# Gated mix of two attention branches, forward and backward: the token stage of the memory branch on the 32x32 blocks of each segment, with compact stores

## The chip, the core and the metric

One core of a Trainium2 chip. The metric is the device time of one launch in microseconds (us), the median of several runs; lower is better. Engines: TensorE (PE, with its weight loads PEld), VectorE (DVE), ScalarE (ACT), GpSimd (POOL) and SyncE (SP, which here only issues DMAs; POOL and ACT issue some too). Each engine takes its instructions in order.

## What is computed

The reference is a forward pass with all its gradients (12 outputs). Two branches read the same x of 2048 tokens with 576 features:

```python
a = _A_ref(x, ...)          # 32 query heads of 18, one key and one value head, softmax over all 2048 tokens
b = _B_ref(x, mem0, ...)    # 32 heads of 128, 64 segments of 32 tokens, one after the other
return g * a + (1 - g) * b  # g = sigmoid(sum(x * gate_w))
```

Branch B is where the change lies. Per segment it computes

```python
h = concatenate([mem, xs])                          # 8 memory rows + 32 tokens
q, k, v = h @ Wq, h @ Wk, h @ Wv                    # per head, 128 wide
scores = where(mask, q @ k.T * scale, -1e9)         # 40 x 40; mask: memory keys always, tokens causal
o = softmax(scores) @ v @ Wo
mem = o[:8]; outs.append(o[8:])                     # the next segment's memory
```

So a token sees 8 memory keys and at most 32 token keys, those of its own segment. The backward pass needs, for each segment and head, P (the softmax), dP = dO v^T less the row sum of dO times o, dS = scale * P * dP, and dq = dS k, dk = dS^T q, dv = P^T dO.

## The kernel before, in words

The program runs in stages: preparation and projections; the forward memory chain (segment by segment, for the memory rows alone), woven with the first pass of branch A; **the token stage** (`b_bulk`); the backward memory chain (`b_chain_bwd`), woven with the second pass of branch A; the backward token stage (`b_post`); the weight gradients (`b_dw`); the end of branch A. Within these stages the order of work on each engine is the order in which the program writes it; a DMA load may be issued somewhat earlier.

*Token stage, `b_bulk`.* 2048 tokens are 16 tiles of 128 rows, that is of 4 segments. A unit of work t (128 of them) is one tile and 4 heads; a chunk is 4 units (16 heads), and loads and stores go by chunks: q, dO, k with four buffers, v with three (L678). A software pipeline runs over ticks. In tick t the list `order` calls one step after the other, each for the unit t - n:

```python
order = [(0, st_QT), (1, st_S), (3, st_T), (4, st_O), (0, st_KT), (2, st_R), (1, st_M), (5, st_OT), (5, st_VT),
         (6, st_D), (0, st_GT), (7, st_B), (8, st_DT), (9, st_Q), (7, st_K)]
```

- `st_QT`, `st_KT`, `st_GT`, `st_VT`, `st_OT`: 4 transposes each on PE (helper `tr`, L87) of q, k, dO, v and o into a PSUM tile `x_tr` (two buffers), copied out by DVE (q, k; L77) or ACT (v, dO at L79, o at L789). `st_OT` also multiplies dO and o on POOL (`x_prod`, L792).
- `st_S`: scores. Per head one product of 128 queries with all 128 keys of the tile (`x_S`; helper `mm`, L82), though three quarters of it belong to other segments, and one with the 4 x 8 memory keys (`x_m`). Two exponentials on ACT (L751, L752) write `x_E`, 160 columns a head.
- `st_M` sets to zero what lies outside the segment and above the diagonal, with a bit mask of 160 columns (DVE, L757). `st_R`: row sums (DVE, L764), reciprocal (L766), P and its memory part Pm (POOL, L769). P with all 128 columns goes to DRAM as `px_dram`.
- `st_T`, `st_DT`: transpose P (and dS). DVE transposes the 4 x 128 columns in 32x32 blocks (L713), which is the whole transpose since only diagonal blocks are not zero; PE transposes the memory part, ACT copies it.
- `st_O`, `st_Q` (through `attend`): o and dq into `x_po` (one buffer): one product of 512 columns with the memory rows in block-diagonal form (`mB`), 4 products of the full 128 x 128 blocks; ACT copies (L723).
- `st_D`: dP into `x_D` as 4 products dO v^T and 4 with a matrix of -1 that subtract the row sums, the same for the memory part in `x_m`; DVE makes dS and dSm (L828); dS goes to DRAM as `dsx_dram`.
- `st_B`: output projection, 8 products of 288 columns. `st_K`: in every second tick 16 products in 32-column tiles for the memory rows' dk and dv (`x_m`; ACT copies `x_dm`, L856).

Stores are collected and issued on SP a tick later (`flush`, L706).

*Who reads the stored blocks.* In `b_chain_bwd`, `kv_load` brings P and dS for the four heads of a step (`r_ks`, L1011), the left operand of the dk and dv products of the last 11 tiles, and `load_a` brings v of the next segment with a transposing DMA (`r_vxT`, L953). In `b_post`, `load` brings P and dS (`y_p`, `y_ds`, L1231) for the first 6 tiles, 8 heads at a time, with three buffers; `y_q` and `y_dO` come beside them (L1233), and `load_s` (L1216, L1219) the memory rows' part.

Of the kernel before, what the change touches and what calls it, by code (L numbers as in the profile page):

```python
# [9 lines left out]
ACT = mybir.ActivationFunctionType  # L10
# [36 lines left out]
class Kern:  # L47
# [52 lines left out]
    def setup_B_dram(self, dram):  # L100
# [20 lines left out]
        self.px_dram = t("px_dram", [NTT, P, HB, P])  # L121
        self.dsx_dram = t("dsx_dram", [NTT, P, HB, P])
# [8 lines left out]
    def setup_B_consts(self, pool):  # L131
# [16 lines left out]
        mz = pool.tile([P, 160], F32, name="maskZ")  # L148
        nc.gpsimd.memset(mz[:], 0.0)
        for sl in range(4):  # L150
            r = slice(32 * sl, 32 * sl + 32)
            nc.gpsimd.memset(mz[r, 32 * sl:32 * sl + 32], 65535.0)
            nc.gpsimd.memset(mz[r, P + 8 * sl:P + 8 * sl + 8], 65535.0)
        nc.gpsimd.affine_select(out=mz[:, 0:P], in_=mz[:, 0:P], compare_op=ALU.is_ge, fill=0.0,
                                base=0, pattern=[[-1, P]], channel_multiplier=1)
        mx = pool.tile([P, 160], U16, name="maskX")
        nc.vector.tensor_copy(mx[:], mz[:])
        self.maskX = mx
        ng = pool.tile([P, 160], BF16, name="negones")
# [485 lines left out]

    def b_bulk(self, wp, lp, sp, psum):
# [49 lines left out]
        def store(t, dst, src):  # L696
            if t % 4 == 3:
                tt, h0 = t // 8, 16 * (t // 4 % 2)
                if len(dst.shape) == 4:
                    due[1].append((dst[tt][:, h0:h0 + 16, :], src[:]))  # L700
                else:
                    due[1].append((dst[tt * P:(tt + 1) * P, h0 * P:h0 * P + 2048], src[:].rearrange("p h e -> p (h e)")))
# [24 lines left out]
        def trans(t, w, nb):  # L727
            tt, g, r, d = view(t)
            pt = psum.tile([P, 5, P], BF16, name="x_tr", bufs=2)
            for i in range(4):  # L730
                self.tr(pt[:, i, :], d[w][:, 4 * (g % 4) + i, :], P)
            o = sp.tile([P, 4, P], BF16, name=f"x_{w}T", bufs=nb)
            self.evac(o[:], pt[:, 0:4, :], use="s" if w in ("dO", "v") else "v")
            sc[w + "T", t] = o
# [6 lines left out]
        def st_S(t):  # L741
            tt, g, r, d = view(t)
            qT4, kT4 = sc.pop(("qT", t)), sc.pop(("kT", t))
            Sp = psum.tile([P, 4, P], F32, name="x_S", bufs=1)
            Sm = psum.tile([P, 4, 32], F32, name="x_m", bufs=1)
            for i in range(4):
                self.mm(Sp[:, i, :], lhsT=qT4[:, i, :], rhs=kT4[:, i, :], start=(i == 0), stop=True)
            for i in range(4):
                self.mm(Sm[:, i, :], lhsT=qT4[:, i, :], rhs=mT[tt]["k"][:, :, 4 * g + i, :], start=(i == 0), stop=True)
            Et = sp.tile([P, 4, 160], BF16, name="x_E", bufs=3)  # L750
            nc.scalar.activation(Et[:, :, 0:128], Sp[:], ACT.Exp, scale=SCALEB)  # L751
            nc.scalar.activation(Et[:, :, 128:160], Sm[:], ACT.Exp, scale=SCALEB)  # L752
            sc["E", t] = Et

        def st_M(t):
            Et = sc["E", t]
            nc.vector.tensor_tensor(out=Et[:].bitcast(U32), in0=Et[:].bitcast(U32),  # L757
                                    in1=mx[:].bitcast(U32).unsqueeze(1).to_broadcast([P, 4, 80]), op=ALU.bitwise_and)

        def st_R(t):  # L760
# [3 lines left out]
            nc.vector.tensor_reduce(out=l[:], in_=Et[:], axis=AX.X, op=ALU.add)  # L764
            rl = sp.tile([P, 4], F32, name="x_r", bufs=2)
            nc.vector.reciprocal(rl[:], l[:])  # L766
            for w, lo, n in (("P", 0, 128), ("Pm", 128, 32)):
                o = chunk(t, w, [P, 16, n], 3)
                nc.gpsimd.tensor_tensor(out=o[:, r, :], in0=Et[:, :, lo:lo + n],  # L769
                                        in1=rl[:].unsqueeze(2).to_broadcast([P, 4, n]), op=ALU.mult)  # L770
            store(t, self.px_dram, d["P"])

        def st_T(t):
            tt, g, r, d = view(t)
            sc["PT", t] = transp(d["P"][:, r, :], d["Pm"][:, r, :], "x_PT", "s")

        def st_O(t):
            tt, g, r, d = view(t)
            o = chunk(t, "o", [P, 16, P], 2)
            attend(o[:, r, :], sc.pop(("PT", t)), mB["v"][t // 4 % 2][:, g % 4], d["v"][:, r, :])  # L780
# [15 lines left out]
        def st_B(t):  # L796
            tt, g, r, d = view(t)
            oT = sc.pop(("oT", t))
            if g == 0:
                pb[tt] = psum.tile([P, 2, 512], F32, name="x_b", bufs=1)  # L800
            for i in range(4):
                for hf in range(2):
                    self.mm(pb[tt][:, hf, 0:288], lhsT=oT[:, i, :], rhs=self.WoN[:, 4 * g + i, 288 * hf:288 * hf + 288],
                            start=(g == 0 and i == 0), stop=(g == 7 and i == 3))
            if g == 7:
# [5 lines left out]
        def st_D(t):  # L811
            tt, g, r, d = view(t)
            prod = sc.pop(("prod", t))
            dOT4 = sc.pop(("dOT", t))
            vT4 = sc.pop(("vT", t))
            dP = psum.tile([P, 4, P], F32, name="x_D", bufs=1)
            dM = psum.tile([P, 4, 32], F32, name="x_m", bufs=1)
            for i in range(4):
                self.mm(dP[:, i, :], lhsT=dOT4[:, i, :], rhs=vT4[:, i, :], start=(i == 0), stop=False)
            for i in range(4):  # L820
                self.mm(dP[:, i, :], lhsT=prod[:, i, :], rhs=self.negones[:, 0:128], start=False, stop=True)
            for i in range(4):
                self.mm(dM[:, i, :], lhsT=dOT4[:, i, :], rhs=mT[tt]["v"][:, :, 4 * g + i, :], start=(i == 0), stop=False)
            for i in range(4):
                self.mm(dM[:, i, :], lhsT=prod[:, i, :], rhs=self.negones[:, 0:32], start=False, stop=True)
            for w, p, src, n in (("dS", "P", dP, 128), ("dSm", "Pm", dM, 32)):
                o = chunk(t, w, [P, 16, n], 2)
                nc.vector.scalar_tensor_tensor(out=o[:, r, :], in0=src[:], scalar=SCALEB,  # L828
                                               in1=d[p][:, r, :], op0=ALU.mult, op1=ALU.mult)
# [1275 lines left out]
```

## Time and profile before

| | |
|---|---|
| runs | 5593.44 us median of 3 (5592.29 to 5598.78) |
| profiled execution | span 5569.0 us from the first to the last instruction; what the runs' median has beyond it is 24.4 us |
| granted PE clock | 0.979 mean; 1.00 in most of the token stage |
| token stage | first scores at 2135.4 us, last at 2775.2 us |
| backward memory chain with pass 2 | some 2810 to 4530 us |
| backward token stage | first product 4536.6 us, last 4774 us |
| weight gradients, end of branch A | from 4788.6 us |

Lines of the profile name the source line, the engine, the operation and the tiles (out<-in). "128*32" ahead of a shape is the part of the PE array in rows and columns that an instruction uses; a product's own length is its way through the array, and products overlap, so start-to-start times tell what one costs.

### The profile page before, as it was taken

Reading aid. Unit: us, or ns where it says so; the run is one execution under the profiler, and the core shown is the slowest. Engines: PE = TensorE matmul, PEld = TensorE weight load, DVE = VectorE, ACT = ScalarE, POOL = GpSimd, SP = SyncE. Lnnn points to the kernel's source line nnn. Section 1 sums busy time; section 2 is a strip of 40 time slices with the busy share of each in tenths; the row PEclk is TensorE's granted clock in tenths of the full one; section 3 lists DMA queues with packets and bytes.
Section 4 is the critical chain, followed back from the end, with each engine's and each line's share of the span. In section 5 each row is a group of like instructions: output and inputs, shape, how many; then the busy total and the mean of one; then the engine's idle time right before and its main releaser. Section 6 shows DMA issues by size and latency. Waiting matters only on the chain. (4 is left out here: it accounts for less than half of the span.)

```text
span 5569.0 us, 204829 instructions
## 1 busy us (share of the span) xinstructions
PE 5231.2 (94%) x87117; PEld 2909.5 (52%) x87117; DVE 3726.0 (67%) x6818; ACT 3506.8 (63%) x5266; POOL 2297.4 (41%) x4320
## 2 busy tenths in 40 slices
PE   7999999999999998999969999999998889899999
PEld 6434444444444445777734555555544457674444
DVE  5337888888888887888868888888888821121111
ACT  4327888788878886888857878878877732111101
POOL 4004555555555545555514544444543421122213
PEclk9999999999999998999979999999999999999999
DMA  6646666766675546888765999999987679876653
GB/s 214 220 173 136 136 138 137 137 138 133 144 135 117 119 99 192 258 256 253 233 228 156 199 200 208 213 202 212 215 181 146 138 181 250 244 214 229 209 165 115
DMA packets 1109896, 1012.49 MB, mean 182 GB/s; under 512 B 666386, under 2 KB 919067, under 8 KB 1099378
## 3 DMA queue, kind: packets, MB, share of 16 engines
q1 hardware_dynamic: 1004706, 747.39, 56.4%
q0 software_dynamic: 100736, 247.10, 14.4%
q8 instruction: 681, 11.16, 0.9%
q10 hardware_dynamic: 3536, 4.90, 0.3%
q14 instruction: 237, 1.94, 0.1%
HBM read 547.90 MB, written 383.13 MB: 167 GB/s over the span
## 5 line engine op out<-in xcount | busy, mean ns | idle before, releaser
L1684 DVE TENSOR_TENSOR a_W<-a_dP,a_E 128x512 bf16<-128x512 f32 x2048 | 1315.1, 684 | 269.9 <-issue 128.7
L1824 DVE TENSOR_TENSOR b_dS<-b_dP,b_E 128x512 bf16<-128x512 f32 x2048 | 1311.8, 684 | 249.3 <-issue 109.0
L1801 ACT ACTIVATE b_E<-b_S 128x1024 bf16<-128x1024 f32 x1024 | 1048.3, 1024 | 308.2 <-PE b_dP L82 237.0
L1654 ACT ACTIVATE a_E<-a_S 128x1024 bf16<-128x1024 f32 x1024 | 1050.0, 1025 | 255.8 <-PE a_dP L82 166.5
L82 PEld LDWEIGHTS <-b_QS 32*128 32x128 bf16 (+1 forms) x8192 | 258.0, 92 | 564.9 <-issue 521.4
L82 PE MATMUL r_pj<-WT,r_dT 128*32 128x288 bf16 x12288 | 496.7, 289 | 17.0 <-issue 16.5
L82 PE MATMUL b_S<-b_KV,b_QS 32*128 32x512 bf16 x2048 | 409.1, 390 | 96.8 <-ACT b_E L1801 77.7
L82 PE MATMUL w_acc<-w_d,w_h 128*128 128x512 bf16 (+1 forms) x2400 | 473.8, 379 | 0.0
L82 PE MATMUL a_S<-a_QD,l_KV 32*128 32x512 bf16 x2048 | 400.3, 384 | 39.5 <-ACT a_E L1654 34.9
L82 PE MATMUL b_acc<-b_dS,b_QS 128*32 128x512 bf16 x2048 | 430.8, 399 | 0.7 <-DVE b_dS L1824 0.5
L82 PE MATMUL b_dP<-b_KV,b_QS 32*128 32x512 bf16 x2048 | 409.8, 394 | 8.2 <-DVE b_dS L1824 8.2
L82 PE MATMUL a_acc<-a_W,l_WK 128*32 128x512 bf16 x4096 | 414.5, 390 | 2.7 <-issue 2.4
L82 PE MATMUL b_acc<-b_E,b_QS 128*32 128x512 bf16 x2048 | 412.8, 400 | 0.0
L82 PE MATMUL a_acc<-a_E,l_VK 128*32 128x512 bf16 x4096 | 405.0, 381 | 5.8 <-issue 1.1
L82 PE MATMUL a_dP<-a_QD,l_KV 32*128 32x512 bf16 x2048 | 399.2, 386 | 0.0
L82 PEld LDWEIGHTS <-r_dT 128*32 128x32 bf16 x12288 | 333.8, 97 | 114.8 <-issue 24.0
L82 PEld LDWEIGHTS <-w_h 128*128 128x128 bf16 (+1 forms) x2688 | 229.8, 100 | 258.8 <-issue 6.9
L82 PEld LDWEIGHTS <-hm 128*32 128x32 bf16 x7680 | 203.9, 97 | 195.0 <-issue 0.8
L769 POOL TENSOR_TENSOR x_P<-x_E,x_r 128x512 bf16<-128x512 bf16 x128 | 152.7, 1193 | 293.6 <-DVE x_r L766 293.6
L79 ACT CAST w_o<-w_acc 128x512 bf16<-128x512 f32 x54 | 31.6, 585 | 384.3 <-PE w_acc L82 365.0
L77 DVE CAST w_o<-w_acc 128x512 bf16<-128x512 f32 x54 | 37.3, 691 | 333.4 <-PE w_acc L82 306.5
L82 PEld LDWEIGHTS <-l_KV 32*128 32x128 bf16 x4096 | 122.0, 91 | 250.6 <-issue 206.2
(461 smaller groups left out, 10953.2 us busy)
## 6 DMA issues: line engine op xcount, KB each, us to landing
b_QS<-qs_dram SPq DMA_DIRECT2D x256, 256.0 KB
dOx_dram<-p_tok SPq DMA_DIRECT2D x16, 1024.0 KB
c_vx<-vx_dram SPq DMA_DIRECT2D x64, 256.0 KB
krow_dram<-c_k POOLq DMA_DIRECT2D x64, 256.0 KB
qrow_dram<-c_q POOLq DMA_DIRECT2D x64, 256.0 KB
vrow_dram<-c_v POOLq DMA_DIRECT2D x64, 256.0 KB
x_q<-qx_dram SPq DMA_DIRECT2D x32, 512.0 KB
x_dO<-dOx_dram SPq DMA_DIRECT2D x32, 512.0 KB
```

The source lines that it names most:

```text
L77: nc.vector.tensor_copy(out, in_)
L79: nc.scalar.copy(out, in_)
L82: return self.nc.tensor.matmul(out, lhsT, rhs, start=start, stop=stop, tile_position=tp, skip_group_check=True)
L769: nc.gpsimd.tensor_tensor(out=o[:, r, :], in0=Et[:, :, lo:lo + n], in1=rl[:].unsqueeze(2).to_broadcast([P, 4, n]), op=ALU.mult)
L1654: nc.scalar.activation(E_[n][:], S.pop(n)[:], ACT.Exp, scale=SCALEA)
L1684: nc.vector.tensor_tensor(out=W_[n][:, i, :], in0=dP[i][:], in1=E_[n][:, i, :], op=ALU.mult)
L1801: nc.scalar.activation(E_[n][:], S.pop(n)[:], ACT.Exp, scale=SCALEA)
L1824: nc.vector.tensor_tensor(out=D_[n][:, i, :], in0=dP[i][:], in1=E_[n][:, i, :], op=ALU.mult)
```

## The change

Scores, dP, P and dS of a segment's tokens are computed, kept and stored as 32x32 blocks only. In detail:

- Scores and dP go to one PSUM tile `x_SD` of one bank, for both the score unit (t - 1) and the dP unit (t - 6) of a tick: the memory products and the row-sum products first (`st_SDm`, full array; the row-sum product now covers token and memory columns at once, 64 columns), then per head and segment a product of 32 queries with 32 keys in one of four 128x32 tiles of the array (`st_SDx`, 32 products).
- `x_E`, P and dS have 32 token and 32 memory columns a head: one exponential, one mask, one sum, one multiplication on POOL, one dS on DVE.
- o and dq: the memory product as before (`attend_m`, all full-array products of a tick together), then per head and segment a 32x32 block times 32 rows, at the array position (32c, 32c) (`attend_x`, 32 products in a tick for both). `x_po` has two buffers.
- Steps are split and sorted so that products of one mode stand together, and the projection's 8 products stand in pairs between the transposes. DVE copies dO's transposes and the two small ones (P, dS), ACT no longer does.
- P and dS are stored as `pd_dram` (32 columns a head). The transposed v is kept by chunk and stored as `vT_dram`, four stores a chunk.
- `b_chain_bwd` loads v's transpose from `vT_dram` with a plain DMA, and P and dS together with four DMAs (one a segment) into the diagonal blocks of two tiles that POOL has set to zero at its start. `b_post` does the same for `y_p` and `y_ds` with four DMAs each, into three tiles each, cleared by POOL and DVE at its start.

```diff
-        self.px_dram = t("px_dram", [NTT, P, HB, P])
-        self.dsx_dram = t("dsx_dram", [NTT, P, HB, P])
+        self.pd_dram = t("pd_dram", [NTT, P, 2, HB, SEG])
+        self.vT_dram = t("vT_dram", [NSEG, P, HB, SEG])
...
+    def load_diag(self, dst, tt, hs, w=slice(0, 2)):
+        for i in range(4):
+            r = slice(32 * i, 32 * i + 32)
+            self.nc.sync.dma_start(dst(r), self.pd_dram[tt][r, w, hs, :])
...
-        def transp(x, m, nm, use):
+        def transp(d, r, nm):
             pt = psum.tile([P, 5, P], BF16, name="x_tr", bufs=2)
-            self.tr(pt[:, 0, :], m.rearrange("p i t -> p (i t)"), P)
-            o = sp.tile([P, 640], BF16, name=nm, bufs=2)
-            nc.vector.transpose(o[:, 0:512], x.rearrange("p i t -> p (i t)"))
-            self.evac(o[:, 512:640], pt[:, 0, :], use=use)
+            self.tr(pt[:, 0, :], d[:, 1, r, :].rearrange("p i t -> p (i t)"), P)
+            o = sp.tile([P, 256], BF16, name=nm, bufs=2)
+            nc.vector.transpose(o[:, 0:128], d[:, 0, r, :].rearrange("p i t -> p (i t)"))
+            nc.vector.tensor_copy(o[:, 128:256], pt[:, 0, :])
             return o
-        def attend(o, PT, m, v):
-            po = psum.tile([P, 4, P], F32, name="x_po", bufs=1)
-            self.mm(po[:].rearrange("p i e -> p (i e)"), lhsT=PT[:, 512:640], rhs=m.rearrange("p i e -> p (i e)"),
+        def attend_m(PT, m):
+            po = psum.tile([P, 4, P], F32, name="x_po", bufs=2)
+            self.mm(po[:].rearrange("p i e -> p (i e)"), lhsT=PT[:, 128:256], rhs=m.rearrange("p i e -> p (i e)"),
                     start=True, stop=False)
+            return po
+        def attend_x(o, po, PT, v):
             for i in range(4):
-                self.mm(po[:, i, :], lhsT=PT[:, 128 * i:128 * i + 128], rhs=v[:, i, :], start=False, stop=True)
+                for c in range(4):
+                    r32 = slice(32 * c, 32 * c + 32)
+                    self.mm(po[r32, i, :], lhsT=PT[r32, 32 * i:32 * i + 32], rhs=v[r32, i, :],
+                            start=False, stop=True, tp=(32 * c, 32 * c))
             nc.scalar.copy(o, po[:])
...
+            if w == "v":
+                o = chunk(t, "vT", [P, 4, 16, SEG], 2)
+                nc.scalar.copy(o[:, :, r, :].rearrange("p s h t -> p h s t"),
+                               pt[:, 0:4, :].rearrange("p h (s t) -> p h s t", t=SEG))
+                if t % 4 == 3:
+                    for c in range(4):
+                        due[1].append((self.vT_dram[4 * tt + c][...], o[:, c]))
+                return
-            self.evac(o[:], pt[:, 0:4, :], use="s" if w in ("dO", "v") else "v")
+            nc.vector.tensor_copy(o[:], pt[:, 0:4, :])
...
-        def st_S(t):
...
-            for i in range(4):
-                self.mm(Sp[:, i, :], lhsT=qT4[:, i, :], rhs=kT4[:, i, :], start=(i == 0), stop=True)
...
+        def seg_mm(dst, lT, rT, first):
             for i in range(4):
+                for c in range(4):
+                    r32 = slice(32 * c, 32 * c + 32)
+                    self.mm(dst[r32, 0, i, :], lhsT=lT[:, i, r32], rhs=rT(i, c), start=False, stop=True, tp=(0, 32 * c))
+        def st_SDm(tick):
+            SD[tick] = psum.tile([P, 2, 2, 4, SEG], F32, name="x_SD", bufs=1)
...
+                    self.mm(SD[tick][:, 0, 1, i, :], lhsT=sc["qT", t][:, i, :], rhs=mT[tt]["k"][:, :, 4 * g + i, :], ...)
...
+                    self.mm(dP[:, 1, i, :], lhsT=dOT4[:, i, :], rhs=mT[tt]["v"][:, :, 4 * g + i, :], ...)
...
+                    self.mm(dP[:, :, i, :], lhsT=prod[:, i, :], rhs=self.negones[:]...)
+        def st_SDx(tick):
...
+                seg_mm(SD[tick][:, 0], qT4, lambda i, c: kT4[:, i, 32 * c:32 * c + 32], True)
+                Et = sp.tile([P, 2, 4, SEG], BF16, name="x_E", bufs=3)
+                nc.scalar.activation(Et[:], SD[tick][:, 0], ACT.Exp, scale=SCALEB)
...
+                seg_mm(SD[tick][:, 1], sc.pop(("dOT", t)), lambda i, c: vT[:, c, 4 * (t % 4) + i, :], False)
+                o = chunk(t, "dS", [P, 2, 16, SEG], 2)
+                nc.vector.scalar_tensor_tensor(out=flat(o[:, :, r, :]), in0=flat(SD[tick][:, 1]), scalar=SCALEB,
+                                               in1=flat(d["P"][:, :, r, :]), op0=ALU.mult, op1=ALU.mult)
+                store_pd(t, 1, d["dS"])
...
-        order = [(0, st_QT), (1, st_S), (3, st_T), (4, st_O), (0, st_KT), (2, st_R), (1, st_M), (5, st_OT), (5, st_VT),
-                 (6, st_D), (0, st_GT), (7, st_B), (8, st_DT), (9, st_Q), (7, st_K)]
+        B_ = lambda i: lambda t: st_B(t, i)
+        order = [(0, st_QT), (7, B_(0)), (0, st_KT), (7, B_(1)), (5, st_OT), (7, B_(2)), (5, st_VT), (7, B_(3)),
+                 (0, st_GT), (4, st_Om), (9, st_Qm), (3, st_T), (None, st_SDm), (8, st_DT), (2, st_R), (7, st_K),
+                 (None, st_SDx), (1, st_M), (4, st_Ox), (9, st_Qx)]
...
-            nc.sync.dma_start_transpose(L["vxT"][:], self.xtok["v"][s * 32:(s + 1) * 32, :])
+            nc.sync.dma_start(L["vxT"][:], self.vT_dram[s])
...
+        kvA = [kvp.tile([P, 2, 4, P], BF16, name=f"r_ks{i}") for i in range(2)]
+        for t in kvA:
+            nc.gpsimd.memset(t[:], 0.0)
...
-            a = kvp.tile([P, 4, P], BF16, name="r_ks", bufs=3)
-            nc.sync.dma_start(a[:], (self.dsx_dram if w else self.px_dram)[tt][:, 4 * g:4 * g + 4, :])
+                self.load_diag(lambda r: kvA[n // 2 % 2][r, :, :, r], tt, slice(4 * g, 4 * g + 4))
...
+        PD = {w: [pool.tile([P, 8, P], BF16, name=f"y_{w}{i}") for i in range(3)] for w, pool in (("ds", rp), ("p", sp))}
+        for i in range(3):
+            nc.vector.memset(PD["ds"][i][:], 0.0)
+            nc.gpsimd.memset(PD["p"][i][:], 0.0)
...
+                if w in PD:
+                    d[w] = PD[w][c % 3]
+                    for i in range(4):
+                        r = slice(32 * i, 32 * i + 32)
+                        nc.sync.dma_start(d[w][r, :, r], self.pd_dram[tt][r, int(w == "ds"), h0:h0 + 8, :])
+                    continue
```

More of the change, by code (lines that the diff above doesn't have):

```diff
@@ L809, in st_B, with st_Qm, st_Qx @@
                 due[1].append((self.b_dram[tt * P:(tt + 1) * P, :], b[:].rearrange("p a b -> p (a b)")))
[L811 to L829, printed above, removed]
[L830 removed]
         def st_DT(t):
             tt, g, r, d = view(t)
[L834 to L836 removed]
+            sc["DT", t] = transp(d["dS"], r, "x_DT")
+        def st_Qm(t):
+            tt, g, r, d = view(t)
+            sc["pq", t] = attend_m(sc["DT", t], mB["k"][t // 4 % 2][:, g % 4])
+        def st_Qx(t):
             tt, g, r, d = view(t)
             dq = chunk(t, "dq", [P, 16, P], 2)
[L839 removed]
+            attend_x(dq[:, r, :], sc.pop(("pq", t)), sc.pop(("DT", t)), d["k"][:, r, :])
             store(t, self.xtok["dq"], dq)
@@ L1966, in build_full @@
             k.setup_A_consts(cpool)
-            k.setup_B_consts(cpool)
+            k.setup_B_consts(cpool, a1s)
             k.load_Wo(bwo)
```

136 lines of the change are left out of this document (79 added, 57 removed).

## The prediction, made before the changed kernel was built

> **What bounds the kernel now.** I read the page first, then the stage table (busy time by window), then the token stage's tiles, its groups by form and its timeline, and last the waits and SP's timeline of the two later stages that read what is stored.
>
> ```profile
> span 5569.0 us, 204829 instructions
> ...
> PE 5231.2 (94%) x87117; PEld 2909.5 (52%) x87117; DVE 3726.0 (67%) x6818; ACT 3506.8 (63%) x5266; POOL 2297.4 (41%) x4320
> ```
>
> The span is 24.4 us under the runs' median of 5593.4; I take that rest as unchanged and add all differences to the median. 0.2% of it, 11 us, is about what a measurement of this kernel can tell from no change. PE is busy everywhere, so the question is what PE does in the stage that is changed.
>
> ```profile
> core 0: us, PE busy (x) PEld busy (x) DVE busy (x) ACT busy (x) POOL busy (x), PEclk, DMA share, GB/s
> ...
> 2300.00:2400.00 100.00, 92.64 (x1423) 76.01 (x1423) 83.03 (x181) 82.48 (x190) 52.12 (x60) 1.00 0.83 256
> ```
>
> ```profile
> L82 PE MATMUL x_S<-x_kT,x_qT x512: 218/219/315, 2135.4 to 2775.2; 128*128 128x128 bf16 x171
> ```
>
> The 128 groups ("ticks") of the token stage take 2775.2 - 2135.4 = 639.8 us for 127 steps: 5.04 us a tick, at full granted clock. PE leads, DVE and ACT are at 83%, the DMA engines too. The timeline of PE shows what a product costs and where PE stands still (start, length, operation, how many):
>
> ```profile
> 2404.88 0.39 PE L82 MATMUL x_po<-x_k,x_DT 128*128 128x128 bf16 x4
> ...
> 2405.20 0.25 PE L82 MATMUL x_m<-x_q,x_dSm 128*32 128x128 bf16 x4
> ...
> 2405.26 0.24 PE L82 MATMUL x_m<-x_dO,x_Pm 128*32 128x128 bf16 x4
> ...
> 2405.37 0.24 PE L82 MATMUL x_m<-x_dO,x_Pm 128*32 128x128 bf16 x4
> ...
> 2405.55 0.40 PE L87 MATMUL x_tr<-identB,x_q 128*128 128x128 bf16 x4
> ...
> 2407.92 0.38 PE L87 MATMUL x_tr<-identB,x_v 128*128 128x128 bf16 x4 [0.28 <-DVE x_kT L77]
> ```
>
> Four full products with 128 columns end their stream after 4 x 0.056 = 0.22 us (0.39 less the 0.22 of one, over 3 steps: 0.056 each). Four products in 32-column tiles start together and the next four 0.057 later: 0.014 us each. Between the modes there is a hole: the first tiled product could start at 2405.11 and starts at 2405.20, the first full one after them could at 2405.43 and starts at 2405.55. From the single start times one change of mode costs 0.095 us. The last line is a standstill: the transpose of v needs a buffer that DVE has not emptied.
>
> Adding up the start-to-start times of 100 ticks gives 4.15 us of streaming in a tick (42 products of 128 columns, 2.35; 12 of 32 columns at 0.025, 0.30; 8 of 288 columns at 0.122, 0.98; 2 of 512 at 0.216, 0.43; 8 tiled, 0.11) and 0.89 of standing: 0.36 before v's transposes, 0.20 before the memory scores, 0.11 before `x_po`, 0.10 before o's transposes, 0.10 in mode changes.
>
> **The change, step by step.**
>
> *PE's streaming.* 22 transposes stay (1.23), the output projection (0.98), the two 512-column products (0.43), the tiled key products (0.11), 8 memory products of 32 columns (0.20). Four products with 128 columns and four with 32 become four with 64: between 0.025 and 0.056 each, nearer the short ones, 0.12. The 4 + 4 full score products become 32 of 32 columns in 128x32 tiles. Their nearest row is the memory chain's:
>
> ```profile
> 2089.67 0.39 PE L82 MATMUL a_S<-a_QD,l_KV 32*128 32x512 bf16 x2
> 2089.67 0.39 PE L82 MATMUL a_dP<-a_QD,l_KV 32*128 32x512 bf16 x2
> 2089.99 0.40 PE L82 MATMUL a_acc<-a_W,l_WK 128*32 128x512 bf16 x4
> ...
> 2090.65 0.41 PE L82 MATMUL c_x<-c_qT,c_kmT 128*8 128x8 bf16 x32
> ```
>
> 32 column-tiled products of 8 columns take 0.41 less one tail of 0.17: 0.0075 us each. 32 columns need hardly more: 0.23 a tick, and at most 0.80 if each held the array for the 0.025 of a 32-column full product. [...]
>
> The 8 products of 128 columns in attention output and dq become 32 in 32x32 tiles on the diagonal, 4 beside each other: 0.014 each as in the column tiles, 0.45. No row has this mode. That four row groups can run together the first two lines above show (four starts within 0.01 us), but each of those writes a PSUM bank of its own, and here four row groups write one. Upper bound: one after the other, 32 x 0.056 = 1.79. I take 0.45, since the diagonal's four write different partitions as the column tiles do. [...]
>
> Sum 3.75. Sorted by mode there are 3 changes a tick (full, 128x32, 32x32, full): 0.29. PE: 4.03 us.
>
> *The other engines.* DVE: the two 128x512 transposes (0.70) shrink to 128x128 (between the 0.20 of `r_xq`, 128x64, and 0.435 of `r_pq`, 128x256: 0.28), the reduce from 640 to 256 elements (0.81 to 0.41 at 1.04 ns each), mask 0.46 to 0.26, dS 0.68 + 0.28 to 0.41; it gains dO's copy (0.42) and two small copies (0.20 each) from ACT. Sum of the rows 4.65 to 3.5. ACT loses those copies and one exponential: 4.7 to 3.1. POOL 2.75 to 1.8. None reaches 4.03.
>
> *What is late next.* With the projection spread between the transposes, PE reaches dO's transposes 1.87 after q's. They need o's buffer: o's transposes end at 1.32, ACT's copy (0.59) ends at 1.95, so 0.12 of standing; in every second tick ACT has also the 0.59 of `x_dm` and runs late by another 0.12. DVE's row from dO's copy to the next q copy (0.34 + 0.36 + 0.36 + 0.51 + 0.33 + 0.18 + 0.42, starts overlapping by 0.08) plus the 1.32 from o's to dO's transposes and the hand-overs is 4.05: just about PE's length, another 0.05 to 0.1 in odd ticks. Tick: 4.2, and 4.25 with the chunk borders. 5.04 - 4.25 = 0.79, times 128 is 101 us; the 9 filling and emptying ticks give half of that, 4 us.
>
> *DMA and SP in this stage.* By the trace's packet records the 16 engines work 4.19 us a tick. Two stores with 128 rows of 4 KB a chunk of four ticks go (64 packets a tick at 201 ns over 16 engines: -0.80), six with 128 rows of 1 KB come (192 at 46 to 62 ns: +0.55 to 0.74): 3.94 to 4.13 a tick, less than 4.25 but close; that is rival B. SP issues four more stores a chunk, 4 x 0.4 = 1.6 us beside 11.5 of 17: hidden; if not, 0.4 a tick.
>
> *Backward memory chain (2810 to 4530).* v comes by a plain load instead of a transposing one (SP 1.6 to 0.45, 64 times) and each pair of blocks by 4 DMAs of 64-byte runs instead of 2 (88 x 2 x 0.5 more on SP): +15 us of SP's time in 1700. 90112 packets of 64 bytes at the 11 ns of the 72-byte ones are 62 us of 16 engines for 87 removed. PE's waits for DMA there sum to under 4 us in 1630, so I take 0, bounds -5 and +15. Two memsets on POOL at the start: +1.
>
> *Backward token stage (4537 to 4774).* Six more DMAs a chunk, 3 us of SP beside idle stretches of 6.5 in 9.6: hidden. But its start hangs on SP: `y_p` went out at 4523.8, the twelve loads behind it, and PE waited 11.0 us for the last. Now POOL must clear the first tile after its last chain DMA (4527) and more loads go ahead: +6, bounds 0 to 15.
>
> Forecast: 5593.4 - 101 - 4 + 1 + 6 = 5495 us.
>
> **The rivals.**
> B, DMA-bound token stage: 4.04 us of transfers at a share of 0.88 (just above the stage's 0.85 now) is a tick of 4.6: -56 - 4 + 7, 5540. Against it: shares up to 1.00 in the backward token stage.
> C, slower: the diagonal products run one by one. 1.79 for 0.45 makes the tick 4.25 + 1.34 = 5.59, and 5.55 where some standing is hidden by it: +65 + 7, 5665. It decides from about 0.040 us a product on. For it: no row shows row groups sharing a bank. Against it: different partitions.
> [...]
> E, the change does not do what it says: the buffer loop of the transposes, not work, sets the tick, and standing grows as streaming shrinks; about 5593 to 5605. Against it: the projection now stands between all of them.
>
> **How the numbers follow.** Forecast 0.65, B 0.11, D 0.06, C 0.12, E 0.06 (0.04 same, 0.02 slower). Faster 0.82, same 0.04, slower 0.14. The range: PE's bare 4.03 gives 5593.4 - 129 - 5 + 1 = 5460; upwards it takes in B and D with the start of the backward token stage at its worse bound, 5575. C and E stay out.
>
> **What would show it.** Right: first to last `x_S` products about 540 us apart; four diagonal products within 0.06 us; three holes of 0.1 a tick; the largest standing at dO's transposes with ACT's o copy as releaser; DMA share above 0.9 with no PE wait on loads. Wrong: diagonal products 0.05 apart (C), score tiles 0.025 apart (D), PE waiting for `x_q`, `x_k` or `x_v` loads (B), a standstill over 0.3 at one transpose (E), or the first `y_pk` more than 20 us after the chain's end.

## The result and the profile after

The changed kernel is slower: 5720.51 us median (5705.96 to 5733.86) against 5592.86 of the kernel before run beside it, a ratio of 1.0233 with an interval of 1.0212 to 1.0254. Forecast were 5495 us and a range of 5460 to 5575. The profiled execution has 135.2 us more than that of before:

```profile
span 5704.2 us, 216189 instructions
...
PE 5236.9 (92%) x92749; PEld 2864.9 (50%) x92749; DVE 3591.4 (63%) x7085; ACT 3334.0 (58%) x4754; POOL 2193.1 (38%) x4190
```

PE's busy time did not grow (5236.9 for 5231.2), the span did: PE stands still more. Where, the first and last products of the stages say. Lengths of stages are compared, since the part ahead of the token stage, which no kernel here changes, ended between 2123.9 and 2155.7 us in the profiles of this study.

| us, first to last start | before | after | difference |
|---|---|---|---|
| token stage, first to last transpose of q | 641.2 | 672.4 | +31.2 |
| last transpose of q to first `b_S` | 43.2 | 41.0 | -2.2 |
| backward memory chain, first `b_S` to first `y_pk` | 1723.1 | 1797.2 | +74.1 |
| backward token stage, first `y_pk` to last `y_pdx` | 237.5 | 259.8 | +22.3 |
| all ahead of the token stage (unchanged) | 2129.1 | 2139.7 | +10.7 |

So the loss lies in three places, and the token stage, forecast 101 us shorter, is one of them. Its row of the stage table (the columns as before: PE, PEld, DVE, ACT, POOL busy, granted clock, DMA share, GB/s) and its scores:

```profile
2300.00:2400.00 100.00, 84.70 (x2214) 66.64 (x2211) 59.08 (x212) 53.95 (x108) 33.81 (x39) 1.00 0.80 239
```

```profile
L82 PE MATMUL x_SD<-x_kT,x_qT x2048: 176/176/210, 2147.4 to 2819.6; 128*32 128x32 bf16 x187
```

Every engine is less busy than before (PE 92.6, DVE 83, ACT 82.5 there), at full clock, and yet (2819.6 - 2147.4) / 127 = 5.29 us a tick. The timeline of two ticks shows why (start, length, operation, how many, idle time before it and its releaser):

```profile
2401.18 0.28 PE L82 MATMUL x_SD<-x_kT,x_qT 128*32 128x32 bf16 x16
...
2401.46 0.59 ACT L899 CAST x_dm<-x_m 128x512 bf16<-128x512 f32 x1 [1.25 <-PE x_SD L82]
...
2401.94 0.39 ACT L797 ACTIVATE x_E<-x_SD 128x256 bf16<-128x256 f32 x1
2402.38 0.28 PE L82 MATMUL x_SD<-x_vT,x_dOT 128*32 128x32 bf16 x16 [0.92 <-ACT x_E L797]
2402.59 0.40 PE L82 MATMUL x_po<-x_v,x_PT 32*32 32x128 bf16 x16
...
2402.82 0.39 PE L82 MATMUL x_po<-x_k,x_DT 32*32 32x128 bf16 x16
...
2407.25 0.28 PE L82 MATMUL x_SD<-x_vT,x_dOT 128*32 128x32 bf16 x16 [0.59 <-ACT x_E L797]
```

Sixteen scores take 0.28 with their tail of 0.18, so 7 ns each; sixteen diagonal products 0.40 with 0.22, or 0.23 from the first group's start to the second's: 14 ns each. Streaming is as forecast. But between the scores and the dP products PE stands for ACT's exponential, 0.59 us, and 0.92 in the ticks where ACT first copies `x_dm`: both halves lie in one tile, `x_SD`, and the dP products may not write it before ACT has read the scores. PE's list of waits for 100 ticks of the stage:

```profile
PE x_SD L82 <- ACT x_E L797: 74.6, 99, 0.9
PE x_tr L87 <- DVE x_dOT L756: 5.5, 13, 0.4
```

In the chain, the waits of PE in the segments 8 to 47, where the blocks are loaded, first of before (window 3094 to 4145), then of after (3134 to 4259):

```profile
PE b_S L82 <- DMA b_QS<-qs_dram: 1.1, 2, 0.9
```

```profile
PE b_S L82 <- DMA b_QS<-qs_dram: 54.7, 33, 3.2
```

Ahead of segment 8 and behind 47 the two kernels run alike (growth 0.1 and -0.8 us). The DMA engines are not fuller there: their share is 0.81 for 0.94. In the backward token stage PE waits 14.5 us for `y_mR` at the start (11.0 before), 12.4 for `h_hist`, 8.6 for `y_dO` and `y_q`.

### The profile page after: what moved, and what is told of

The parts are those of the page before. It is cut to its first block, busy times and chain, and to the rows that moved or that the text cites. A ratio compares the mean times of both kernels' runs of the same rounds, so it can differ in the third digit from the quotient of the medians.

```text
span 5704.2 us, 216189 instructions
## 1 busy us (share of the span) xinstructions
PE 5236.9 (92%) x92749; PEld 2864.9 (50%) x92749; DVE 3591.4 (63%) x7085; ACT 3334.0 (58%) x4754; POOL 2193.1 (38%) x4190
## 4 chain that ended last, share of the span: by engine, by line
PE 42%; issue 6%; ACT 6%; DMA 6%; POOL 1%; SPq 1%; DVE 0%; ACTq 0%; POOLq 0%; DVEq 0%
PE w_acc L82 11%; PE r_pj L82 6%; PE b_S L82 5%; PE b_acc L82 4%; PE r_x L82 4%; ACT b_E L1859 4%; DMA b_QS<-qs_dram 3%; PE x_tr L87 3%; PE x_po L82 2%; PE x_b L82 2%; PE x_SD L82 1%; ACT x_E L797 1%; PE f_big L82 1%; PE z_pt L87 0%; PE x_m L82 0%
## 5 line engine op out<-in xcount | busy, mean ns | idle before, releaser
L1859 ACT ACTIVATE b_E<-b_S 128x1024 bf16<-128x1024 f32 x1024 | 1049.1, 1025 | 387.5 <-PE b_dP L82 259.8
L851 POOL TENSOR_TENSOR x_prod<-x_dOT,x_oT 128x512 bf16<-128x512 bf16 x128 | 148.0, 1157 | 316.5 <-ACT x_oT L848 312.0
```

The source lines that it names most:

```text
L851: nc.gpsimd.tensor_tensor(out=sc["prod", t][:], in0=sc["dOT", t][:], in1=oT[:], op=ALU.mult)
L1859: nc.scalar.activation(E_[n][:], S.pop(n)[:], ACT.Exp, scale=SCALEA)
```

## Experiments

Theory 1: the wait on the exponential took the token stage's gain. Theory 2: SP issues its DMAs in order, and the four loads of blocks per pair delay what stands behind them, `b_QS` above all. Each run's ratio is to the kernel before on the same chip; its medians beside these runs were 5567 to 5589 us, for 5593 above, so a time and its expectation can lie some 20 us apart by this alone, and the ratio tells more.

**Both product groups ahead of the exponential.**

```
 seg_mm(SD[tick][:, 0], qT4, ...)          # scores
+seg_mm(SD[tick][:, 1], dOT, ...)          # dP, moved up
 nc.scalar.activation(Et[:], SD[tick][:, 0], ACT.Exp, scale=SCALEB)
-seg_mm(SD[tick][:, 1], dOT, ...)
```

> The changed kernel with one edit in the token stage: both groups of sixteen 32-row products into x_SD (scores of one tick, dP of another) are issued on PE one behind the other, ahead of ACT's exponential that reads the scores; before, the exponential stood between them, and PE was idle 0.92 us a tick in front of the dP products until ACT had read the scores out of the shared x_SD tile. Theory 1 (the token stage lost its gain to that wait): the tick falls from 5.29 us to 4.25-4.5, 127 ticks give 100 to 130 us less than the changed kernel (5720 to about 5600), and the wait at x_SD<-x_vT,x_dOT on ACT x_E goes to under 0.1 us a tick; the chain and the stage behind it keep their +74 and +22 us. Rival (the many small products themselves, or the DMA queues, hold the tick): the wait moves to another product, the tick stays above 5.0 us, and the time within 30 us of 5720.

Measured: 5675.08 us, ratio 1.0169 (1.0145 to 1.0193). The wait is gone, and the token stage is 630.0 us long, 42 less than in the changed kernel and 11 less than before, with a mean tick of 4.96. So theory 1 names a real term, but 0.92 us a tick went (by start times; 0.75 in the list above, which leaves out the last score's way through the array) and only 0.33 were won; both expectations miss. Half of the ticks are under 4.68 us, the others reach 8.3. What stands in those is taken up below.

**The diagonal loads on POOL's queue, and, apart from it, the `b_QS` loads there.**

```
-self.nc.sync.dma_start(dst(r), self.pd_dram[...])      # first run
+nc.gpsimd.dma_start(dst(r), self.pd_dram[...])
-nc.sync.dma_start(QS[:], self.qs_dram[p, q4])          # second run
+nc.gpsimd.dma_start(QS[:], self.qs_dram[p, q4])
```

> The changed kernel, where the four loads per pair of the diagonal blocks (r_ks<-pd_dram, 352 of them in the backward memory chain) are issued on POOL's queue instead of SP's; the same bytes in the same 64-byte runs. Theory 2 (SP issues in order, the four 0.71 us issues per pair stand ahead of the b_QS loads, and PE waits for b_QS 55 us): the chain's growth of 74 us falls to under 25, b_QS waits to under 10 us, the time to about 5650-5670. Rival 2a (the 64-byte runs are slow in the DMA engines, whatever queue issues them): growth stays above 55 us, time 5710-5730. Rival 2b (any issue of 352 more DMAs costs, wherever it is): the growth stays because POOL now delays the chain's own steps, seen as waits on POOL lines and not on b_QS. The token stage and the last stage stay as in the changed kernel.

> The changed kernel, where only the 128 b_QS loads are issued on POOL's queue instead of SP's; the diagonal loads stay on SP as they are. Theory 2: b_QS is late only because it is issued behind the diagonal loads, so its wait falls from 55 us to under 10 and the chain's growth from 74 us to under 30 (POOL takes the issue of 128 DMAs); time about 5650-5680. Rival 2a (64-byte runs slow in the DMA engines): b_QS stays late by its landing, growth above 55 us. Rival 2c (not b_QS but the other loads of the chain on SP are what is late): the b_QS wait goes and another SP load takes its place, growth above 55 us.

Measured: 5739.41 us (1.0282, 1.0248 to 1.0317) and 5741.28 us (1.0288, 1.0263 to 1.0314); the chain takes 1817 and 1829 us, longer still than the 1797 of the changed kernel. PE's waits in the first run:

```profile
PE b_dP L82 <- DVE b_dS L1882: 68.9, 43, 3.7
```

`b_QS` is in time (in the median of every second chunk, which is one `b_QS` load, its issue is 10.3 us ahead of its use, for 5.5 in the changed kernel), and PE waits for DVE instead: POOL, 693 us busy in that window for 507, holds up steps of the chain that DVE's queue waits for (DVE stands 86.5 us for POOL's `r_dspad`, a wait that the changed kernel does not have). That is rival 2b. In the second run (256 loads, not the 128 of its expectation) PE waits 69.2 us for `b_QS`, more than in the changed kernel. POOL does not issue it late; it lands late: where PE had to wait, the product starts 7.1 us behind the issue in the median, for 5.0 with SP's queue. Why was not tried. Neither run tells 64-byte runs from the count of issues; both only move the queue.

**Four loads per pair of 256-byte runs, and one.** P and dS are loaded into a tile without zeros and multiplied block by block:

```
-self.load_diag(lambda r: kvA[n // 2 % 2][r, :, :, r], tt, heads)   # 4 DMAs, 64-byte runs
+nc.sync.dma_start(ks[:], self.pd_dram[tt][:, :, heads, :])         # 1 DMA; first run: 4, of 32 partitions
-self.mm(pk[:, i, :], lhsT=a[:, i, :], rhs=b[:, i, :], ...)
+for c in range(4):
+    self.mm(pk[r, i, :], lhsT=a[r, i, :], rhs=b[r, i, :], ..., tp=(32 * c, 32 * c))
```

> The changed kernel, where the backward memory chain loads P and dS compact, into a tile of 32 columns a head, with the same count of four DMAs per pair on SP, but runs of 256 bytes instead of 64; the products there read sixteen 32x32 blocks (four row and column groups) instead of four 128x128 tiles with zeros beside the blocks. Theory 2 in the form 'the count of issues decides': an issue takes about the same 0.6-0.7 us, the growth of 74 us stays within 25 us of that, time 5700-5740. Rival 2a (the 64-byte runs decide, in the issue or in the DMA engines): an issue falls to 0.5 us or less and the growth to under 35 us, time 5660-5690. The sixteen products, by 14 ns each in the token stage of the changed kernel against four of 55 ns, should cost PE about nothing. The last stage still loads into zeroed tiles and keeps its +22 us.

> The changed kernel, where the backward memory chain and the stage behind it load P and dS compact with one DMA (256-byte and 512-byte runs) instead of four with 64-byte runs, and multiply them as sixteen 32x32 blocks instead of four 128x128 tiles with zeros. Theory 2 (SP's in-order issues: four per pair stand ahead of b_QS): with one issue per pair, less than the two of the kernel before, the b_QS waits of 55 us go under 15, the chain's growth of 74 us against the kernel before under 25, and the growth of 22 us in the last token stage under 10; time 5640-5665. Rival 2d (PE's own instruction stream: the sixteen products add some 4,000 products and weight loads to the chain, and PE stands with nothing to wait for but an instruction block that lands late, as in 25 waits of the run with four compact loads): b_QS waits go but PE's waits on issue grow to over 40 us, growth 40-70 us, time 5685-5715.

The first run has the four loads in the chain alone; the second has one load a pair in the chain and, in the backward token stage, one load each for P and dS of a chunk. Measured: 5723.08 us (1.0255, 1.0226 to 1.0283), and 5606.81 us (1.0071, 1.0048 to 1.0095). SP's issues of these loads (count, duration in ns: least, median, longest) in before, after, with four and with one:

```profile
L1011 SPq DMA_DIRECT2D r_ks<-px_dram x88: 320/442/1952, 2977.4 to 4116.9; - x88
```

```profile
L651 SPq DMA_DIRECT2D r_ks<-pd_dram x352: 557/612/1979, 3019.4 to 4236.0; - x176
```

```profile
L1062 SPq DMA_DIRECT2D r_ks<-pd_dram x352: 538/593/1925, 3021.0 to 4245.6; - x176
```

```profile
L1060 SPq DMA_DIRECT2D r_ks<-pd_dram x88: 571/581/1380, 3011.0 to 4158.6; - x88
```

Before there were two lines like the first, 176 issues. An issue cost 0.6 us whether its runs had 64 or 256 bytes, and whether it filled 32 partitions or 128; the loads of before, with runs of 1 KB, cost 0.44. With 352 issues the chain is 1807 us long, with 88 it is 1731 (before: 1723). The two runs have the same products, so the count of issues is the cause, and the form "the count decides" of theory 2 stands. The `b_QS` waits are gone with one load. Rival 2d falls: PE's waits in the chain with no releaser ("issue") are 24 us, under its 40, and the chain has grown by 8 (with the four loads they are 37, and the waits for `b_QS` 31). In the backward token stage one load for four took the length from 259.8 to 240.3; only the 11.9 us for `y_mR` are left:

```profile
PE y_pk L82 <- DMA y_mR<-qrow_dram: 11.9, 1, 11.9
PE y_pk L82 <- DMA y_dO<-dOx_dram: 1.0, 1, 1.0
```

**Both together, and a fourth `b_QS` buffer.**

```
-QS = sp.tile([P, 2, 512], BF16, name="b_QS", bufs=3);  load(n // 4 + 2)
+QS = sp.tile([P, 2, 512], BF16, name="b_QS", bufs=4);  load(n // 4 + 3)     # second run alone
```

> The reordered token stage and the compact loads together, in the changed kernel. If the two are independent, the time is 5720 less 45 (what the reordering gave) less what the compact loads give alone: theory 2 5595-5620, rival 2d 5640-5670.

> The kernel with the reordered token stage and the compact loads, with b_QS in four buffers instead of three and loaded three chunks ahead instead of two (some 12 us more of lead). Theory 2: what is left of the b_QS waits goes to zero and the chain is no slower than in the kernel before (growth 0 to 10 us); 10 to 30 us less than the same without the fourth buffer if waits were left there, the same if none were. Rival 2d: the b_QS waits are gone, and the chain stays 40 us or more longer than in the kernel before, since PE waits for instruction blocks.

Measured: 5556.12 us, ratio 0.9986 (0.9971 to 1.0002), and 5563.81 us, 0.9990 (0.9977 to 1.0002). The chain takes 1721.5 and 1723.2 us, as before: nothing was left for the fourth buffer (its chunk more is 6.6 us of lead, 1700 us over 256, not the 12 of the expectation). With both causes removed the kernel is level with before, not 100 us faster; what is missing is in the token stage (618.9 and 631.4 us).

**What stands in the long ticks.** The timeline of PE in the combined kernel shows one, and below it the stage table for the same stretches (PE busy first, granted clock third from the end):

```profile
2411.73 0.19 PE L82 MATMUL x_SD<-x_kT,x_qT 128*32 128x32 bf16 x3
2414.48 0.29 PE L82 MATMUL x_SD<-x_kT,x_qT 128*32 128x32 bf16 x13 [2.55 <-issue]
...
2414.80 0.61 PE L82 MATMUL x_po<-x_v,x_PT 32*32 32x128 bf16 x16
```

```profile
2405.00:2411.00 6.00, 5.66 (x120) 4.02 (x120) 3.47 (x12) 3.39 (x7) 2.36 (x3) 1.00 0.86 229
2412.00:2414.00 2.00, 0.00 (x0) 0.00 (x0) 0.33 (x2) 0.58 (x1) 0.61 (x1) 0.97 0.69 236
2414.50:2418.00 3.50, 3.50 (x78) 2.91 (x79) 1.47 (x4) 1.46 (x3) 0.00 (x0) 0.50 0.84 259
```

PE stops between the third and the fourth of sixteen like products, with no operand outstanding. The trace's DMA records have a queue for instructions, and there a block of 16 KB ended at 2413.06, 1.42 us before PE goes on. Counted over the stage, without its first 25 us or so, in which the pipeline fills (stands: starts over 0.8 us apart; "behind a block": such a block ended 1.2 to 1.55 us before, a window that covers 4 to 7% of the time):

| token stage | PE instructions a us | blocks | PE instructions / 256 | stands, us | behind a block, us |
|---|---|---|---|---|---|
| before | 28.5 | 67 | 66.8 | 0 | 0 |
| after | 43.3 | 108 | 108.2 | 65, 66.3 | 7, 7.3 |
| reordered | 46.3 | 108 | 108.6 | 18, 32.6 | 14, 26.7 |
| both together | 46.9 | 108 | 108.2 | 19, 26.3 | 19, 26.3 |
| mask moved | 46.1 | 108 | 108.1 | 30, 53.8 | 28, 51.3 |
| zero products added | 51.6 | 138 | 137.1 | 60, 99.1 | 53, 91.8 |
| P spread | 42.4 | 97 | 97.0 | 18, 31.2 | 13, 24.6 |
| P and dS spread | 36.1 | 86 | 86.0 | 107, 99.5 | 4, 3.9 |

One block came for each 256 products and weight loads of PE. That gives theory 3: PE uses up its instructions faster than their blocks come. The last four rows are the runs that follow, and one more, which was to lower the count and failed:

```
-nc.vector.transpose(o[:, 0:128], P_blocks)                     # sixteen 32x32 products per head group
+for c in range(4): nc.vector.transpose(z[r32, :, r32], P[r32])  # z: 128x128 with zeros, four products
```

> The kernel with the reordered token stage, where the products into x_po read P and dS transposed from 128x128 tiles with zeros beside the blocks (four products of 128 columns instead of sixteen of 32x32, twice a tick); DVE writes the blocks with four transposes of 32 rows instead of one of 128. PE's column time stays (4 x 55 ns against 16 x 14 ns), its products fall from about 115 to 91 a tick, and two changes of tiling mode go. Theory 3 (in the reordered kernel PE runs 4.4 and 4.7 us ticks, but stands up to 3.9 us in some because a 16 KB block of its instructions lands late, with 45 products and as many weight loads a us): the long ticks become rare, the mean tick falls from 4.96 to 4.3-4.6 us, 45 to 80 us less than the reordered kernel (5675 to about 5595-5630). Rival 3a (DVE, which gains some 1 us a tick, becomes the bound): ticks of an even 4.7-5.0 us without holes, time within 25 us of 5675. Rival 3b (the holes have another cause): the holes stay as long and as many, 5645-5675.

Measured: 5895.97 us, ratio 1.0594 (1.0566 to 1.0622), an even tick of 6.8. A transpose of 32 rows took as long as one of 128, here in this run and then in the changed kernel (mean ns behind the bar):

```profile
L729 DVE STREAM_TRANSPOSE x_PT<-x_P 32x128 bf16<-32x128 bf16 x174 | 52.3, 300 | 1.8
```

```profile
L722 DVE STREAM_TRANSPOSE x_PT<-x_P 128x128 bf16<-128x128 bf16 x98 | 29.5, 301 | 0.0
```

Six more of them are 1.8 us a tick, and the mask of `x_E` took 0.61 us for 0.28: DVE holds the tick, worse than rival 3a had it (PE waits 95 us for it in 300, and it is itself 77% busy), and the run says nothing on theory 3. Its expectation counts 45 products and as many weight loads a us; the 46 of the table are both together.

**Two buffer waits removed.** In the combined kernel PE still stands 0.24 us a tick ahead of o's transposes and 0.18 ahead of dO's, by the start times.

```
-(None, st_SDx), (1, st_M), (4, st_Ox)            +(0, st_KT), (2, st_M), (7, B_(1))     # both runs
-(0, st_GT), (4, st_Om), (9, st_Qm), (3, st_T)    +(4, st_Om), (9, st_Qm), (0, st_GT), (3, st_T)   # first run alone
```

> The kernel with the reordered token stage and the compact loads (5556 us against 5567 of the kernel before, ratio 0.9986), and two more moves in the token stage's order: DVE's mask of x_E goes from the end of a tick to behind the copy of x_kT in the next, so that the copies of x_qT and x_kT, whose x_tr buffers the transposes of o wait for (0.24 us a tick), come 0.4 us earlier; and PE's transposes of dO (0.18 us a tick of standing, for ACT's copy of x_oT) go behind the two products of 512 columns into x_po. Theory 4 (PE sets the tick through these two buffer waits): the standing at o and dO falls under 0.1 us each, the tick from 4.83 to 4.4-4.6 us in the mean, 30 to 50 us less: 5505-5530, ratio to the kernel before 0.989-0.994. Rival 4a (the wait moves to the transposes of P, which then wait for x_vT or x_dOT): the tick stays 4.75 or more, 5540-5560.

> The same without the second move: only the mask of x_E goes behind the copy of x_kT. Theory 4: the standing at the transposes of o falls from 0.24 to under 0.1 us a tick, that at dO stays at 0.17; 15 to 30 us less than without the move: 5526-5541. Rival 4a: the wait moves to the transposes of v or dO and nothing is gained, 5550-5560.

Measured: 5584.07 us, 0.9998 (0.9985 to 1.0010), and 5581.71 us, 0.9988 (0.9977 to 1.0000). In both the stand at o's transposes is gone, and in the first run that at dO's too, but there a stand of 0.33 came ahead of the transpose of dS, as rival 4a had it, though not for P. The median tick fell from 4.69 us to 4.55 and 4.58, the mean did not (4.87 to 4.96 and 4.95): theory 4's times miss. The stands behind blocks went from 26 us to 35 and 51. The combined kernels with three and four `b_QS` buffers have the same token stage; their stands behind blocks are 26 and 32 us, and its length differs by 12.5 us. So the growth is not shown to come from the moves.

**More instructions, and fewer.**

```
+for i in range(4):
+    for c in range(4):      # zeros into x_po, after each attention product
+        self.mm(po[r32, i, 0:8], lhsT=zeros[r32, 0:32], rhs=zeros[r32, 0:8], ..., tp=(32 * c, 32 * c))
```

> The kernel with the reordered token stage and the compact loads, and thirty-two products of zeros a tick more on PE (8 columns each, into x_po, which they leave as it is), so that PE's instruction stream in the token stage grows by 64 a tick, some 28%, and its column time by 32 products of at most 14 ns, 0.2 to 0.45 us a tick. Theory 3 (the irregular long ticks are instruction blocks that land late): PE's stands of over 0.7 us behind such a block grow from 19 (24 us) to over 30 (over 45 us), and the tick by the column time and 0.15 us or more of stands: 5610-5660. Rival 3c (the stands come with the data transfers and not with the rate of instructions): 15 to 25 stands of 20 to 35 us as before, and the tick grows by the column time alone, 5580-5615.

Measured: 5678.56 us, ratio 1.0177 (1.0155 to 1.0198); the stands rise from 19 to 60, and those behind a block from 26 to 92 us. The mean tick is 5.59 for 4.87, and (99.1 - 26.3) / 127 = 0.57 of these 0.72 are stands. Theory 3 holds and rival 3c falls. Then the other way, with the spreading of the blocks given to ACT and POOL:

```
+for c in range(4):
+    (nc.scalar.copy if c < 2 else nc.gpsimd.tensor_copy)(z[r32, :, r32], transposed[r32])
-16 x self.mm(po[r32, i, :], lhsT=PT[r32, ...], rhs=v[r32, i, :], tp=(32 * c, 32 * c))
+ 4 x self.mm(po[:, i, :], lhsT=z[:, i, :], rhs=v[:, i, :])
```

> The kernel with the reordered token stage, the compact loads and the mask behind the copy of x_kT (5582 us against 5585 of the kernel before, mean tick 4.95, median 4.58, 31 stands of over 0.7 us), where the transposed blocks of P and dS are spread into 128x128 tiles with zeros by four copies of 32 rows each, two on ACT and two on POOL, and x_po takes four products of 128 columns instead of sixteen of 32x32, twice a tick. PE's instructions fall by 48 a tick, some 21%, its column time stays, and DVE keeps its work; ACT and POOL, 54% and 34% busy in the changed kernel, gain about 0.6 us each per attention product, 1.2 a tick. Theory 3 (instruction blocks that land late hold the tick): stands of over 0.7 us fall to under 10, mean tick 4.3-4.6 us, 45 to 80 us less: 5505-5540, ratio to the kernel before 0.986-0.992. Rival 3d (ACT's or POOL's in-order queue becomes the bound, since the copies stand ahead of the exponential): even ticks of 4.8-5.3 without stands behind blocks, 5565-5630.

> The same for the products of P alone, those of dS stay sixteen of 32x32: PE's instructions fall by 24 a tick, ACT and POOL gain some 0.6 us a tick each. Theory 3: stands fall from 31 to 10-20, mean tick 4.5-4.75, 25 to 55 us less: 5530-5560. Rival 3d: less of the loss than with both, 5565-5600.

Measured: 5595.94 us, ratio 1.0011 (1.0000 to 1.0023), for P and dS; 5571.45 us, ratio 0.9968 (0.9953 to 0.9984), for P alone. With both, the stands behind blocks shrink to 4 us, as theory 3 says, but the tick is an even 5.0: rival 3d. The list of waits of all engines names ACT's queue and DVE's behind it:

```profile
PEld L87 <- ACT x_o L756: 79.5, 117, 1.2
PE x_tr L87 <- DVE x_qT L774: 78.8, 116, 1.2
```

With P alone the stage is the shortest of all, 612.5 us, though by less than the 12.5 us by which the same stage differed above, and PE at its fullest of these kernels:

```profile
2300.00:2400.00 100.00, 91.88 (x2093) 72.14 (x2113) 62.14 (x226) 67.69 (x155) 47.54 (x81) 0.97 0.84 247
```

This version beats both: by 0.32% the kernel before, and, by the two ratios (0.9968 / 1.0233), by 2.6% the changed one. That it beats the combined kernel (0.9986) is not shown, as the two intervals overlap. It misses its expectation of 5530 to 5560; 25 us of stands behind blocks remain.

## Why the prediction was wrong

*PE's streaming* was right: 3.75 us a tick forecast, 3.72 by the start times of 100 ticks of the changed kernel. Score tiles at 7 ns (7.5) refute rival D. The 25 ns for each score tile on which that rival, and through it the range's upper end, rests, no run shows: 25 ns is what a 32-column product of the full array took from start to start in before and after (medians), and the tiles took 7. Diagonal products at 14 ns (14) refute rival C: the row groups ran beside each other though they write one tile, `x_po` (four started within 10 ns of each other in the median). *The changes of mode* cost 0.094 to 0.133 against 0.095, and *dO's transposes* 0.18 within 0.12 to 0.24.

*What is late next* is the step that failed first. I followed the buffers of the transposes and forgot the tile that the change itself introduced: scores and dP had a tile each, now they share one, with ACT's exponential between them. It cost 0.75 us a tick in the 100 ticks above. Rival E came nearest, since standing grew as streaming shrank, but its place was the transposes.

The same step failed a second time, in a resource that it did not look at. Once that wait is gone, PE needs 46 instructions a us for 28.5, and their delivery takes part of the gain; no page of before shows it, as before has no such stand. I counted products by column time and never by number. Delivery is not all of it: the combined kernel's mean tick is 4.87 for the forecast 4.25, and of these 0.62 the stands behind blocks are 0.21 (26.3 us over 127 ticks). Another 0.24 stands ahead of o's transposes, for which the sum had no term; the rest is not taken apart. With the shared tile well ordered the forecast gain of 105 us was 10 to 22 us in this stage (631.4 to 618.9 for 641.2).

*Backward memory chain 0, bounds -5 and +15*: 74.1. The count was right (four issues for two), an issue was 0.61 us in the median and 0.71 in the mean for a mean of 0.50, and SP's queue did not fill (its issues took 907 us of the 1125 of that window, for 792 of 1051 before). Wrong was the reading that it is hidden because PE's waits for DMA were under 4 us before: `b_QS` is issued two chunks ahead in the same in-order queue, in before 6.9 us ahead of its use in the median and 5.6 in the lowest tenth (every second chunk counted), and the waits come where under 5 us are left (2 of 80 before, 29 of 80 after, for 2 and 33 waits). There were 0.6 to 1.9 us of slack, and the burst added 4 x 0.71 - 2 x 0.50 = 1.8 a pair. *Backward token stage +6*: 22.3, of which +3.5 by the later start, within the bounds, and the rest from loads in the stage that I called hidden.

*DMA* stayed off the path (share 0.80 for 0.83): rival B falls. The range's upper end, 5575, took in none of this, because both causes of loss were called covered on the ground of idle time in sum, without the lead of each transfer.

## What to carry to other kernels

When a product group is moved into a shared tile, write down who reads each half and when, and issue both halves ahead of the first reader (the stage went from 672.4 to 630.0 us by it). `b_QS` was hidden here by its lead over its use at the moment of the burst (2 waits before, 33 after, where under 5 us were left), not by idle time of its queue in the sum: count the issues ahead of a transfer. Splitting the attention products into smaller tiles kept PE's column time (four at 56 ns, sixteen at 14), and with the other splits PE's instructions rose from 28.5 to 43.3 a us; in this stage stands behind their blocks were 4 us at 36 a us, 25 to 51 at 42 to 47 and 92 at 52 (7 at 43 in the changed kernel, where PE stood for the exponential), so take the split only where it saves columns.

## What the hardware showed that was not expected

PE's instructions came in blocks of 16 KB, one for 256 products and weight loads (the pages count 681 blocks for 2 x 87117 before and 726 for 2 x 92749 after), and PE stood when one ended late: in the combined kernel it went on from all 19 stands of the token stage, 26.3 us, 1.2 to 1.55 us after the end of a block. At 28.5 instructions a us, before, no such stand was seen; at 46.3 and 46.9 (reordered, both together) there were 14 and 19. The late blocks were not slow: in the combined kernel the 19 took 0.99 us each in the median, the others 1.04. What was late is their start; whether they stood behind data (the DMA share is 0.84 there) or were asked for late was not tried.

In the chain a stand cost more than itself. In the segments 8 to 47 of the changed kernel all 16 stands of 2.1 us and more are followed by a granted clock of 0.50 to 0.77 in the next 3 us (mean 0.60); of the 7 between 1.5 and 2 us four kept 1.00. The rows of the segments 8 to 47, before and after, show what this comes to:

```profile
3094.00:4145.00 1051.00, 1008.34 (x21097) 543.05 (x21096) 877.71 (x1523) 845.17 (x1125) 506.02 (x925) 0.98 0.94 207
```

```profile
3134.00:4259.00 1125.00, 1037.95 (x21101) 548.06 (x21091) 881.19 (x1521) 845.21 (x1125) 507.43 (x925) 0.95 0.81 179
```

With the same products PE is busy 29.6 us longer, at a mean clock of 0.95 for 0.98, and all the waits in its lists sum to 83.3 us for 38.9. These 29.6 and 44.4 are the 74 of the chain, so by this sum two fifths of its loss are the clock's. With one load for four the waits for `b_QS` and the loss of clock are both gone (PE 1012.2 us busy, clock 0.99). The length of a stand does not decide alone: in the run with `b_QS` on POOL's queue three of nine stands of 2.1 us and more in the chain were followed by 1.00. In the token stage of the combined kernel one of three such stands was followed by 0.50 and two by 1.00.

A DVE transpose of 32 partitions took the 0.30 us of one of 128 (300 ns with four transposes for one, 301 in the changed kernel), and SP's issue of a load 0.6 us with runs of 64 as of 256 bytes, into 32 partitions as into 128 (medians 612, 593 and 581 ns).

Not settled: whether the wait in `x_SD` goes by the tile or by its PSUM bank. Two tiles in two banks were not tried.
